# Sigmoid attention in rounds of two pairs of heads: rest keys of both pairs on four 64x64 tiles, queries and keys split from SBUF

## The chip, the core and the metric

One NeuronCore of a Trainium2 chip runs the kernel. The engines named below are TensorE (PE; PEld are its weight loads), VectorE (DVE), ScalarE (ACT), GpSimd (POOL) and SyncE (SP, which issues most DMAs). The metric is the device time of one execution, in microseconds; the kernel before takes 999.67 us (median of three, 999.48 to 1000.31).

## What is computed

Attention with a sigmoid in place of the softmax, over 4 batches of 12 heads with 448 tokens of 64 features, and then two dense layers, each with an inner width of 2048:

```python
scores = scale * np.matmul(q, k.transpose(0, 1, 3, 2)) - np.log(S)
attn = 1.0 / (1.0 + np.exp(-scores))
x = np.matmul(attn, v)              # (4, 12, 448, 64) -> (1792, 768)
h = x @ w_in;  x = np.where(h > 0, h, np.exp(np.minimum(h, 0)) - 1) @ w_out
h = x @ w_in2; x = (h - np.tanh(h)) @ w_out2
```

q, k and v are float32, the weights float64.

## The kernel before

Attention goes by pairs of heads (`pairs`, 24 of them, six per batch). The 448 keys of a head are 3 x 128 keys and a rest of 64 (`RS`). For pair n the kernel does this:

- **Loads.** `ld_qk` brings queries and keys into `raw_qk` (SP's queue); GpSimd puts the two heads side by side into `ql` and `kl` (`side_by_side`, L230), which waits for the transposes of pair n - 2. `ld_kr` and `ld_vr` bring the rest keys and rest values of four pairs at once (`NR`), two DMAs each; `krest` holds head 0 and head 1 in a block diagonal with zeros in the other corners. `ld_v` brings the values of two pairs (`NL`).
- **Transposes** (`transpose`, L299, TensorE): four for the keys (the fourth is the rest), four for the queries, into PSUM.
- **Split.** Each operand becomes two float32r numbers, a head and a rest: `head` (keys on ScalarE, L305; queries on VectorE, L307) copies from PSUM into `es[n % 2]`, and `rest` (VectorE, L312) subtracts the head from the PSUM tile. `es` has two copies, one per parity of the pair.
- **Scores** (`scores`, L334): for each block u of 128 keys three matmuls (head x rest, head x head, rest x head) per head, the two heads on the two 64-row halves of the array. Block u = 3 is the 64 rest keys of both heads on all 128 rows, three matmuls into the bank `psq`. The three score buffers `pss` have two banks each.
- **Sigmoid** (`sig`, L348, ScalarE) on 2 x 448 columns, and on 448 for the rest keys.
- **Values** (`pv`, L359): float32, head 0 into PSUM partitions 0 to 63 and head 1 into 64 to 127 (two column tiles of 128x64); a float32 matmul appears as two instructions in the trace. For u = 3 the rows of `vrest` that belong to the other head are zero.
- **Result** (`xdone`, L371, VectorE) from `psv` into the R tiles, the input of the first dense layer.

TensorE's order in steady state is scores of pair n, transposes of pair n + 2, values of pair n; its tiling goes from 64x128 to 128x128 to 128x64 in each pair.

`Sched` makes the order: every operation has a queue, a cost, what it waits for, and a rank, which in attention is a due time from `PHASES` (nanoseconds from the start of a pair, `CYCLE` apart). Attention is planned first, alone. The dense layers' operations are then put between on all engines, but an operation on ScalarE or VectorE that would delay a planned one of attention by more than `GIVE` is put off. During attention this other work is the narrowing of the float64 weights (`narrow_to`, L534 on ScalarE, L537 and L541 on VectorE), the sums and stores of the first layer's output weights (`p_sum`, L594; `p_store`, L599), whose due times are two `CYCLE`s apart, and, as results come in, the operands of the first products (`x_sum`, L695; `x_head`, L705; `x_rest`, L711; `w_head` and `w_rest`, L668 and L671). The first products (`m_p`, L739) follow the last `pv` on TensorE in a fixed order (`sequence`), 128 rows by 128 columns.

## Time and profile before

| | |
|---|---|
| median of three runs | 999.67 us |
| span of the profiled execution | 997.6 us |
| TensorE busy | 985.6 us (99%) |
| VectorE busy | 763.5 us (77%) |
| ScalarE busy | 601.3 us (60%) |
| GpSimd busy | 105.1 us (11%) |
| TensorE's granted clock | 90% of full speed or more in each of the page's 40 slices |

The profiled execution has its span only, first instruction to last; its time outside the span isn't listed. Busy time is the time in which an engine had at least one instruction running. Records of one engine may overlap: an instruction's recorded time reaches into the next one's start. The weights, the queries, keys and values stream in during the first 125 us, in which the DMA engines are busy nearly throughout.

### The profile page before, as it was taken

How to read it: one execution, taken by the hardware profiler on the slowest of the kernel's cores; microseconds unless marked ns; L12 is line 12 of the kernel's file. 1: busy time of each engine (PE TensorE's matmuls, PEld its weight loads, DVE VectorE, ACT ScalarE, POOL GpSimd, SP SyncE). 2: the span in 40 equal slices, each digit the busy share in tenths (PEclk: the TensorE clock that was granted, in tenths of full speed). 3: DMA queues.
4: the chain of work that ended last, by engine and by line, in shares of the span. 5: the costliest groups of instructions: out<-in, count | busy, mean ns of one | idle time of the engine just before them, and what ended most of it. 6: DMA issues, size and time to landing. Idle time of an engine off the chain costs nothing.

```text
span 997.6 us, 15554 instructions
## 1 busy us (share of the span) xinstructions
PE 985.6 (99%) x5294; PEld 853.5 (86%) x5294; DVE 763.5 (77%) x1155; ACT 601.3 (60%) x966; POOL 105.1 (11%) x118
## 2 busy tenths in 40 slices
...
GB/s 298 294 353 366 307 140 47 56 200 193 193 192 185 188 253 343 396 358 392 379 261 148 231 75 179 178 182 191 196 189 183 323 323 147 126 172 174 127 144 83
DMA packets 144190, 218.60 MB, mean 219 GB/s; under 512 B 21040, under 2 KB 102512, under 8 KB 143856
## 3 DMA queue, kind: packets, MB, share of 16 engines
...
## 4 chain that ended last, share of the span: by engine, by line
PE 96%; DVE 2%; ACT 1%; DMA 0%; issue 0%; SPq 0%; DVEq 0%
PE psa L739 13%; PE psd L739 11%; PE psx L739 10%; PE pvps L359 8%; PE psu L894 7%; PE psv L894 7%; PE psw L894 7%; PE psa L894 6%; PE psb L894 6%; PE psb L739 5%; PE sps L334 5%; PE psy L894 5%; PE psx L894 3%; PE spq L334 2%; PE sps L299 2%; PE psd L894 1%
## 5 line engine op out<-in xcount | busy, mean ns | idle before, releaser
L348 ACT ACTIVATE an<-sps,bias 128x896 f32<-128x896 f32 x72 | 67.6, 1006 | 36.7 <-PE sps L334 36.5
L866 ACT ACTIVATE XB<-t 128x384 fp32r<-128x384 f32 (+1 forms) x111 | 61.9, 562 | 35.1 <-PE psw L894 8.1
L870 DVE TENSOR_TENSOR XB<-t,XB 128x384 fp32r<-128x384 f32 (+1 forms) x111 | 68.1, 624 | 11.2 <-ACT XB L866 11.1
L654 POOL TENSOR_TENSOR second<-second 128x384 f32<-128x384 f32 x15 | 19.0, 1264 | 539.8 <-DVE second L541 406.7
L359 PE MATMUL pvps<-an,vl 128*64 128x448 f32 x288 | 59.4, 548 | 0.0
L334 PEld LDWEIGHTS sps<-e 64*128 64x128 f32 x432 | 39.8, 190 | 19.8 <-PE pvps L359 11.3
L866 ACT ACTIVATE XB<-spare 128x512 fp32r<-128x512 f32 (+1 forms) x72 | 40.9, 573 | 25.8 <-PE psw L894 10.4
L739 PE MATMUL psa<-XB,W 128*128 128x512 f32 x192 | 54.2, 391 | 0.0
L334 PE MATMUL sps<-e 64*128 64x448 f32 x432 | 52.2, 383 | 0.2 <-DVE e L312 0.2
L870 DVE TENSOR_TENSOR XB<-spare,XB 128x512 fp32r<-128x512 f32 (+1 forms) x72 | 44.0, 621 | 7.9 <-ACT XB L866 7.5
L894 PE MATMUL psu<-XB,XB 128*128 128x384 f32 (+1 forms) x192 | 46.3, 348 | 0.0
L894 PE MATMUL psv<-XB,XB 128*128 128x384 f32 (+1 forms) x192 | 46.2, 348 | 0.0
L894 PE MATMUL psw<-XB,XB 128*128 128x384 f32 (+1 forms) x192 | 46.2, 348 | 0.0
L739 PEld LDWEIGHTS psa<-XB,W 128*128 128x128 f32 x192 | 36.0, 188 | 7.5
L768 ACT ACTIVATE spare<-t 128x512 f32<-128x512 f32 (+1 forms) x33 | 19.0, 579 | 36.9 <-DVE t L756 35.9
L359 PEld LDWEIGHTS pvps<-an,vl 128*64 128x64 f32 x288 | 18.5, 136 | 26.0 <-issue 20.1
L654 POOL TENSOR_TENSOR first<-first,second 128x384 f32<-128x384 f32 x30 | 40.1, 1335 | 1.2
L307 DVE CAST e<-sps 128x448 fp32r<-128x448 f32 x24 | 15.0, 623 | 30.8 <-PE sps L299 23.6
L230 POOL COPY first<-raw_qk 128x384 f32<-128x384 f32 (+1 forms) x44 | 25.0, 573 | 117.4 <-PE sps L299 92.6
L739 PE MATMUL psd<-XB,W 128*128 128x512 f32 x144 | 35.7, 391 | 1.5 <-DVE W L671 1.3
L772 ACT ACTIVATE spare<-spare 128x512 f32<-128x512 f32 (+1 forms) x64 | 36.6, 572 | 0.7
L894 PE MATMUL psa<-XB,XB 128*128 128x384 f32 (+1 forms) x156 | 36.9, 347 | 0.0
...
## 6 DMA issues: line engine op xcount, KB each, us to landing
...
```

The source lines that it names most:

```text
L230: nc.gpsimd.tensor_copy(out=(ql, kl)[w][:, n % NL].rearrange("p c (h d) -> p c h d", h=2), in_=x)
L299: nc.tensor.transpose(ps[:, c * P:(c + 1) * P], x, ident[:P, :P])
L334: nc.tensor.matmul(out=ps[:, j, :S], lhsT=e[lanes, ks, cols], rhs=e[lanes, qs, :S], start=(x == 0), stop=(x == 2),)
L348: nc.scalar.activation(out=a[:, :m], in_=T.pop(("s", n, u))[:, :m, :S], func=ACTF.Sigmoid, bias=bias, scale=scale)
L359: nc.tensor.matmul(out=ps[D * j:D * j + D], lhsT=vl[n // NL % NVL][:, n % NL, 3 * j + u] if u < 3 else vrest[n // NR % 2][:, n % NR, j], r ...
L654: by.tensor_tensor(out=out, in0=x, in1=y, op=op)
L739: nc.tensor.matmul(out=ps, lhsT=w[wz][:, k0:k0 + 128], rhs=xs[xz][:, kk], start=(opens and n == 0), stop=(n == 3 * KH - 1), skip_group_che ...
L768: nc.scalar.activation(out=r, in_=h, func=ACTF.Tanh)
L772: nc.scalar.activation(out=r, in_=r, func=ACTF.Exp, scale=-1.0)
L866: nc.scalar.activation(out=at_place(og_place[i, s, p, j], 0, i)[:, :HW[s]], in_=T["graw", i, s, p, j], func=ACTF.Copy)
L870: nc.vector.tensor_tensor(out=lo, in0=T.pop(("graw", i, s, p, j)), in1=f(hi), op=ALU.subtract)
L894: nc.tensor.matmul(out=T["o2", tag], lhsT=lhsT, rhs=rhs, start=(p in OPENS and j == 0 and x == 0), stop=(j == NG - 1 and x == 2), skip_gro ...
```

## The change

Attention goes in rounds of two pairs (`ROUND`). Within a round TensorE does the scores of the first pair, the transposes of both pairs of the next round, the scores of the second pair, the values of both, the rest values of both (`pv_rest`) and the rest scores of both pairs of the next round (`scores_rest`).

- The rest scores are four plain float32 matmuls of 64x64, one per head, on the four quarters of the array, into one score buffer. They take the place of six float32r matmuls. One sigmoid over 2 x 448 columns takes the place of two over 448. The rest values are four matmuls of 64x64 without the zeros; the results of both pairs stand in one tile of two banks, `T["o", m]`, in which the second pair's heads are crossed: partitions 64 to 127 of a bank hold the other pair's head.
- Because of that crossing the first layer's input weights are loaded with the upper 64 rows of neighbouring blocks exchanged, as three DMAs (`load` for `("wi", 0)`).
- The transposes of a pair go into one tile of two banks (the even pair's with the rest keys of both pairs). One copy brings it as float32 into `plain` in SBUF: on VectorE for the even pair (960 columns), on ScalarE for the odd one (832); for pair 0 both engines share it. From there VectorE makes head (`hi`) and rest (`lo`), each over queries and 3 x 128 keys at once, 832 columns. Even transposes use the result's tile, so they wait for both results of the round before; odd ones use a score buffer.
- The bank `psq` is gone; two of the three score buffers lie in the early pool. `an` has five buffers for three. `ld_kr` and `ld_vr` are four DMAs each, all on SP; the zero fills of `krest` and `vrest` are gone.

The diff, cut to its core (a line of "..." marks what is left out):

```diff
-CYCLE = 6900
+CYCLE = 6000
...
+ROUND = 2 * CYCLE
 PHASES = {
-    ("s", 0): 0, ("s", 1): 620, ("s", 2): 1240, ("s", 3): 1900,
-    ("t", 1): 3100 - 2 * CYCLE, ("t", 0): 3500 - 2 * CYCLE, ("pv", 0): 4000, ("pv", 1): 4900, ("pv", 2): 5800, ("pv", 3): 6500,
-    ("sig", 0): 700, ("sig", 1): 1700, ("sig", 2): 2700, ("sig", 3): 3700,
-    ("head", 1): 4400 - 2 * CYCLE, ("head", 0): 4900 - 2 * CYCLE,
-    ("rest", 1): 5050 - 2 * CYCLE, ("rest", 0): 5700 - 2 * CYCLE, ("xdone",): CYCLE + 500,
-    ("ldk",): 4000 - 5 * CYCLE, ("ldqk",): 1000 - 4 * CYCLE, ("side", 1): 4500 - 3 * CYCLE, ("side", 0): 4600 - 3 * CYCLE, ("ldv",): 3300 - 2 * CYCLE,
+    "s": ((0, 600, 1200), (3900, 4500, 5100)), "sig": ((1100, 2100, 3100), (5100, 6100, 7100)),
+    "pv": ((5900, 6650, 7400), (8150, 8900, 9650)), "pvr": 10500, "xdone": (11400, 12000),
+    "sr": -700, "sigr": 50,
+    "t": (2000 - ROUND, 2900 - ROUND), "plain": (2950 - ROUND, 4100 - ROUND), "hi": (4100 - ROUND, 5800 - ROUND), "lo": (4700 - ROUND, 6400 - ROUND),
+    "side": (4500 - 2 * ROUND, 6000 - 2 * ROUND), "ldqk": (7000 - 3 * ROUND, 8500 - 3 * ROUND),
+    "ldk": 5000 - 3 * ROUND, "ldv": 1500 - ROUND,
 }
...
+SHIFTS = {(0, "ldv"): -12000, (0, "sr"): 2550, (0, "sigr"): 2600, (0, "ldvr"): -11000}
...
-    NAN, NAF, NVL, NL, NR = 3, 1, 2, 2, 4
+    NAN, NVL, NL, NR = 5, 2, 2, 4
...
+            plain = [ld_p.tile([128, w], F32, name=f"plain{i}") for i, w in enumerate((DD + EW, EW))]
+            es = [e0.rearrange("p a t -> p (a t)"), ld_p.tile([128, 2 * EW], F32R, name="e1")]
...
+            def rests(w, g):
+                return heads[w][2 * NR * g:2 * NR * (g + 1), KW:S]
 
             def ld_kr(g):
-                for j in range(2):
-                    nc.sync.dma_start(out=krest[g % 2][RS * j:RS * j + RS, :, D * j:D * j + D], in_=rest_of(0, g, j))
+                for y in range(NR):
+                    i, x = divmod(y, 2)
+                    nc.sync.dma_start(
+                        out=krest[g % 2][RS * x:RS * x + RS, i].rearrange("p (h d) -> p h d", h=2),
+                        in_=rests(0, g)[2 * y:2 * y + 2].rearrange("h p d -> p h d"),
+                    )
 
             def ld_vr(g):
-                for j in range(2):
-                    (nc.sync if g else nc.scalar).dma_start(out=vrest[g % 2][RS * j:RS * j + RS, :, j], in_=rest_of(1, g, j))
+                for z in range(2):
+                    for x in range(2):
+                        nc.sync.dma_start(
+                            out=vrest[g % 2][RS * z:RS * z + RS].rearrange("p (i x) d -> x p i d", x=2)[x],
+                            in_=rests(1, g).rearrange("(i x h) p d -> x h p i d", x=2, h=2)[x, z ^ x],
+                        )
...
+            def transpose(n):
+                ps = t_flat(n)
+                for c in range(3):
+                    nc.tensor.transpose(ps[:, DD + c * 128:DD + (c + 1) * 128], kl[:, n % NL, c], ident)
+                if n % 2 == 0:
+                    nc.tensor.transpose(ps[:, :DD], krest[n // NR % 2][:, n // 2 % 2], ident)
                 for c in range(R):
-                    x = krest[n // NR % 2][:, n % NR] if w and c == 3 else t[:, n % NL, c]
-                    nc.tensor.transpose(ps[:, c * P:(c + 1) * P], x, ident[:P, :P])
-
-            def head(n, w):
-                W, slot = ((S, 1), (512, 2))[w]
-                to, x = es[n % 2][:, slot, :W], T["t", n, w][:, :W]
-                if w:
-                    nc.scalar.activation(out=to, in_=x, func=ACTF.Copy)
+                    nc.tensor.transpose(ps[:, DD + KW + c * SP:DD + KW + (c + 1) * SP], ql[:, n % NL, c], ident[:SP, :SP])
+
+            def parts_of(n):
+                lo, hi = DD * (n % 2), DD + EW
+                return [("ACT", lo, DD + KW), ("DVE", DD + KW, hi)] if n == 0 else [(("DVE", "ACT")[n % 2], lo, hi)]
+
+            def to_plain(n, x):
+                by, lo, hi = parts_of(n)[x]
+                at = DD * (n % 2)
+                out, in_ = plain[n % 2][:, lo - at:hi - at], t_flat(n)[:, lo:hi]
+                if by == "ACT":
+                    nc.scalar.activation(out=out, in_=in_, func=ACTF.Copy)
                 else:
-                    nc.vector.tensor_copy(out=to, in_=x)
-
-            def rest(n, w):
-                W, slot, to = ((S, 1, 0), (512, 2, 3))[w]
+                    nc.vector.tensor_copy(out=out, in_=in_)
+
+            def kq(n):
+                return plain[n % 2][:, DD * (1 - n % 2):][:, :EW]
+
+            def hi(n):
+                nc.vector.tensor_copy(out=es[n % 2][:, :EW], in_=kq(n))
+
+            def lo(n):
                 e = es[n % 2]
-                nc.vector.tensor_tensor(
-                    out=e[:, to, :W], in0=T.pop(("t", n, w))[:, :W], in1=f(e[:, slot, :W]), op=ALU.subtract
-                )
+                nc.vector.tensor_tensor(out=e[:, EW:2 * EW], in0=kq(n), in1=f(e[:, :EW]), op=ALU.subtract)
...
+            def scores_rest(m):
+
+                ps = buffer("sr", m)
+                for x in range(2):
+                    for j in range(2):
+                        lanes, c = slice(64 * j, 64 * j + 64), 64 * (j ^ x)
+                        nc.tensor.matmul(
+                            out=ps[c:c + 64, j, :S], lhsT=plain[0][lanes, RS * x:RS * x + RS], rhs=kq(x)[lanes, KW:], start=True, stop=True,
+                        )
+
...
             def pv(n, u):
-                if u == 0:
-                    T["o", n] = psv.tile([128, 512], F32, tag="o", name="pvps")[:, :S]
-                ps = T["o", n]
-
+                m, x = divmod(n, 2)
+                if (x, u) == (0, 0):
+                    T["o", m] = pso.tile([128, 2, BK], F32, tag="o", name="pvps")
                 a = T.pop(("a", n, u))
                 for j in range(2):
                     nc.tensor.matmul(
-                        out=ps[D * j:D * j + D], lhsT=vl[n // NL % NVL][:, n % NL, 3 * j + u] if u < 3 else vrest[n // NR % 2][:, n % NR, j],
-                        rhs=a[:, j if u < 3 else 0], start=(u == 0), stop=(u == 3),
+                        out=T["o", m][D * j:D * j + D, j ^ x, :S], lhsT=vl[m % NVL][:, x, 3 * j + u], rhs=a[:, j], start=(u == 0), stop=False,
                     )
...
+            def pv_rest(m):
+                a = T.pop(("a", m))
+                for x in range(2):
+                    n = 2 * m + x
+                    for j in range(2):
+                        lanes = slice(64 * (j ^ x), 64 * (j ^ x) + 64)
+                        nc.tensor.matmul(
+                            out=T["o", m][D * j:D * j + D, j ^ x, :S], lhsT=vrest[n // NR % 2][lanes, n % NR], rhs=a[lanes, j], start=False, stop=True,
+                        )
...
-                        op("side", n, (w,), "POOL", 1400, side_by_side, [("ldqk", n, w), ("t", n - NL, w)])
-                    op("t", n, (w,), "PE", (420, 440)[w], transpose, loaded("qk"[w], n) + before_s(n - 2, 3))
-                    op("head", n, (w,), ("DVE", "ACT")[w], (620, 600)[w], head, [("t", n, w)] + used)
-                    op("rest", n, (w,), "DVE", (620, 690)[w], rest, [("head", n, w)])
-                for u in range(4):
-                    m2 = width(u) == 2
-                    op("s", n, (u,), "PE", 660, scores, [("rest", n, 0), ("rest", n, 1)] + (before_s(n, u) if u < 3 else [("sig", n - 1, 3)]))
-                    was = ("pv", *divmod(3 * n + u - NAN, 3)) if m2 else ("pv", n - NAF, u)
-                    op("sig", n, (u,), "ACT", 1010 if m2 else 640, sig, [("s", n, u), was])
-                for u in range(4):
-                    op("pv", n, (u,), "PE", 820, pv, [("sig", n, u)] + (loaded("v", n) + [("xdone", n - 1)] if u == 0 else []))
-                before = [("narrow", 3, 2), ("keep", 2, ("wi", 0, 2)), ("keep", 3, ("wi", 0, 3))] if n == 2 * NP else []
-                op("xdone", n, (), "DVE", 680 if pairs[n][0] == 2 else 630, xdone, [("pv", n, 3)] + before)
+                        sch.op(("side", n, w), "POOL", 800, lambda n=n, w=w: side_by_side(n, w), [("ldqk", n, w), ("t", n - NL)], when("side", n) - w)
+                outs_free = [("xdone", n - 4), ("xdone", n - 3)]
+                op(("t", n), "PE", (1000, 850)[x], transpose, loaded("qk", n) + (free_of(("t", n)) if x else outs_free))
+                for y, (by, c0, c1) in enumerate(parts_of(n)):
+                    op(("plain", n, y), by, int(1.06 * (c1 - c0)) + 120 if by == "DVE" else int(0.87 * (c1 - c0)) + 190, to_plain, [("t", n), ("sr", m - 1), ("lo", n - 2)])
+                op(("hi", n), "DVE", 600, hi, copied(n) + [("s", n - 2, u) for u in range(3)])
+                op(("lo", n), "DVE", 1020, lo, [("hi", n)])
+                for u in range(3):
+                    op(("s", n, u), "PE", (800, 750)[x] if u == 0 else 600, scores, [("lo", n)] + free_of(("s", n, u)))
+                    op(("sig", n, u), "ACT", 1010, sig, [("s", n, u), ("pv", *divmod(3 * n + u - NAN, 3))])
+                    opens = copied(2 * m + 2) if (x, u) == (0, 0) and 2 * m + 2 < NPR else []
+                    op(("pv", n, u), "PE", 900 if (x, u) == (0, 0) else 740, pv, [("sig", n, u)] + loaded("v", n) + opens)
+                if x:
+                    op(("sr", m), "PE", 760, scores_rest, copied(n - 1) + copied(n) + free_of(("sr", m)))
+                    op(("sigr", m), "ACT", 1010, sig_rest, [("sr", m), ("pvr", m - 1)])
+                    op(("pvr", m), "PE", 850, pv_rest, [("sigr", m), ("ldvr", n // NR)] + [("pv", n - y, 2) for y in range(2)])
+                    before = [("narrow", 3, 2), ("keep", 2, ("wi", 0, 2)), ("keep", 3, ("wi", 0, 3))]
+                    for y in (n - 1, n):
+                        op(("xdone", y), "DVE", 680 if pairs[y][0] == 2 else 630, xdone, [("pvr", m)] + (before if y == 2 * NP else []))
...
+                    nc.sync.dma_start(out=to[:64], in_=rows.rearrange("(k z p) f -> z p k f", z=2, p=64)[0])
+                    for x in range(2):
+                        nc.sync.dma_start(
+                            out=to[64:].rearrange("p (m x) f -> x p m f", x=2)[x],
+                            in_=rows.rearrange("(m x z p) f -> x z p m f", x=2, z=2, p=64)[1 - x, 1],
+                        )
...
-            sch.chain([("pv", last, 3)] + sequence)
+            sch.chain([("pvr", NPR // 2 - 1)] + sequence)
```

## Rows read from the trace of the kernel before

**Rows 1.** the page: busy time by engine; the chain that ended last

```profile
PE 985.6 (99%) x5294; PEld 853.5 (86%) x5294; DVE 763.5 (77%) x1155; ACT 601.3 (60%) x966; POOL 105.1 (11%) x118
...
PE 96%; DVE 2%; ACT 1%; DMA 0%; issue 0%; SPq 0%; DVEq 0%
```

**Rows 2.** windows: length, busy us (instructions) per engine, clock, DMA share, GB/s

```profile
9.00:26.20 17.20, 16.13 (x93) 9.55 (x92) 7.26 (x13) 9.50 (x12) 4.48 (x8) 1.00 1.03 350
26.20:162.40 136.20, 136.20 (x902) 81.27 (x900) 112.06 (x194) 106.27 (x143) 20.50 (x36) 1.00 0.80 269
162.40:174.50 12.10, 12.10 (x76) 6.30 (x74) 8.38 (x15) 10.30 (x16) 0.00 (x0) 1.00 0.11 34
174.50:200.70 26.20, 24.72 (x119) 21.16 (x118) 25.25 (x41) 18.77 (x36) 5.05 (x4) 1.00 0.16 61
200.70:997.00 796.30, 789.62 (x4084) 729.35 (x4083) 609.65 (x891) 454.39 (x759) 71.95 (x56) 1.00 0.63 216
```

**Rows 3.** timeline of TensorE, one pair: start, us, engine, line, out<-in, count

```profile
80.73 2.09 PE L334 MATMUL sps<-e 64*128 64x448 f32 x18
82.75 0.88 PE L334 MATMUL spq<-e 128*128 128x448 f32 x3
83.46 0.49 PE L299 MATMUL sps<-ident,first 128*128 128x128 f32 x3
...
83.90 0.55 PE L299 MATMUL sps<-ident,first 112*128 112x112 f32 x4
84.38 2.48 PE L359 MATMUL pvps<-an,vl 128*64 128x448 f32 x12
86.68 0.92 PE L359 MATMUL pvps<-a,vrest 128*64 128x448 f32 x4
87.53 0.47 PE L334 MATMUL sps<-e 64*128 64x448 f32 x2
```

**Rows 4.** the same in narrower windows: TensorE, and its weight loads

```profile
81.64 1.17 PE L334 MATMUL sps<-e 64*128 64x448 f32 x10
...
84.81 0.14 PEld L359 LDWEIGHTS pvps<-an,vl 128*64 128x64 f32 x2 [0.23 <-ACT an L348]
85.18 0.14 PEld L359 LDWEIGHTS pvps<-an,vl 128*64 128x64 f32 x2 [0.23 <-issue]
```

**Rows 5.** timeline of VectorE in the same stretch

```profile
87.65 0.62 DVE L371 COPY R0b<-pvps 128x448 f32<-128x448 f32 x1 [0.53 <-PE pvps L359]
88.19 0.95 DVE L541 SCALAR_TENSOR_TENSOR XB<-XB 128x768 int32<-128x768 int32 x1
89.06 0.69 DVE L711 TENSOR_TENSOR XA<-R0a,XA 128x512 fp32r<-128x512 f32 x1
89.66 1.02 DVE L594 TENSOR_TENSOR XB<-XB 128x384 f32<-128x384 f32 x2
91.31 0.62 DVE L307 CAST e<-sps 128x448 fp32r<-128x448 f32 x1 [0.63 <-PE sps L299]
91.85 0.55 DVE L594 TENSOR_TENSOR XB<-XB 128x384 f32<-128x384 f32 x1
92.60 1.22 DVE L312 TENSOR_TENSOR e<-sps,e 128x512 fp32r<-128x512 f32 x2 [0.20 <-ACT e L305]
```

**Rows 6.** VectorE's shift by lines; the timeline where GpSimd and VectorE meet

```profile
L537 DVE TENSOR_SCALAR XB<-XB 128x768 int32<-128x768 int32 x16 | 8.4, 550 | 0.0
...
112.22 0.62 POOL L230 COPY first<-raw_qk 112x512 f32<-112x512 f32 x1 [0.37 <-DMA raw_qk<-in_q_dram]
112.29 1.08 DVE L711 TENSOR_TENSOR XA<-R0b,XA 128x512 fp32r<-128x512 f32 x1
```

**Rows 7.** timeline: SP at the start; VectorE ahead of the end

```profile
7.85 1.29 SPq L237 DMA_DIRECT2D krest<-in_k_dram  x2
...
170.90 0.55 DVE L711 TENSOR_TENSOR R0b<-R1a,R0b 128x384 fp32r<-128x384 f32 x1
...
173.26 0.56 DVE L711 TENSOR_TENSOR R0b<-R1a,R0b 128x384 fp32r<-128x384 f32 x1 [0.62 <-ACT R0b L705]
```

170 lines of the change are left out of this document (84 added, 86 removed).

## The prediction

> **What bounds the kernel now.** I read the page first: TensorE is busy 985.6 us of a span of 997.6, and the chain that ended last is 96% TensorE with 2% VectorE [rows 1]. So a change pays only where it shortens TensorE's own list, and only for as long as nothing else ends later. Next the windows, cut where the stages begin [rows 2]. Attention in steady state is the window from 26.2 to 162.4: twenty pairs in 136.2 us, TensorE never idle, so 6.81 us a pair and 13.62 for two. VectorE is busy 112.06 there, 82%. The reader should then look at the two windows behind. In the last two pairs VectorE has air (8.38 of 12.10). In the 26.2 us after attention's end, where the operands of the first products are still being split, it is busy 25.25, or 96%, while TensorE idles 1.48. There VectorE is already the bound, and whatever it has not finished when attention ends is added to the time one for one. Behind 200.7 TensorE is at 99% and VectorE at 77%: a microsecond won ahead of that point stays won.
>
> The timeline of one pair shows what TensorE spends [rows 3]: scores 80.73 to 82.75 (2.02), rest scores to 83.46 (0.71), transposes to 84.38 (0.92), values to 86.68 (2.30), rest values to 87.53 (0.85), 6.80 in all. Narrower views give the pace inside [rows 4]. Two 64-row score matmuls go side by side: ten take 1.11 us including the change at their end, eighteen 2.02, so a slot of two is 0.20 and about 0.1 is lost at each end. The float32 matmuls with values are two instructions each, and a slot of two column tiles is 0.375 (weight loads at 84.81 and 85.18): eight slots are 3.00 of 3.15, the change costs 0.15. Transposes are 0.11 (128 columns) and 0.095 (112), with 0.10 at the change. A change of tiling thus costs 0.15 to 0.20, and two pairs have six.
>
> **TensorE, part by part, for a round of two pairs.** Scores: the same 18 slots, 18 x 0.2025 = 3.65. Transposes: 15 for 16, seven at 0.11 and eight at 0.095, 1.53. Values: 12 slots x 0.375 = 4.50. Rest values: four matmuls 64x64, eight instructions; if four tiles run at once, two slots, 0.75 where two pairs now spend 1.50. Rest scores: four plain float32 matmuls, 0.75 by the same slot where two pairs now spend 1.42. Changes: into scores 0.20, to transposes 0.20, back 0.20, to values 0.15, to the 64x64 tiles 0.15, none between rest values and the next rest scores: 0.90. Sum 12.08 against 13.62, **1.54 less a round**; a little under half of it is rest values, a little under half rest scores, the remainder changes and the lost transpose.
>
> Ten such rounds give 15.4. The last round has no transposes: 3.65 + 4.50 + 0.75 and three changes of 0.5 together are 9.4; three score buffers now serve seven uses in a row there, so I put 0.6 on it for sigmoids that come late, 10.0 against 12.10 [rows 2]: 2.1. At the start SP issues four DMAs for the rest keys where two took 1.29 us [rows 7], and four for the rest values that ScalarE's queue carried; the loads of pairs 2 and 3 queue behind these, some 3.9 us later (six issues of 0.65), and GpSimd and the second transposes wait for them. Against it stands one shorter round. I take zero, with 2 us either way. TensorE's list is shorter by **17.5 us** at attention's end.
>
> **VectorE, which must keep up.** Its records overlap by 0.08, so I take start to start [rows 5]: 448 columns 0.54 (87.65 to 88.19 and 91.31 to 91.85), 384 columns 0.47, 512 0.60, 768 0.87: 1.04 ns a column on 0.07. Now a pair costs 0.54 (queries' head) + 1.14 (two rests) + 0.54 (copy of the result) = 2.22, a round 4.44. After: one copy of 960 columns out of PSUM 1.07; two heads of 832; two rests of 832 at 0.94; two result copies at 0.54. The head reads and writes SBUF, which no float32 row here does in this form. The nearest is the 768-column shift, one SBUF source, 0.55 [rows 6] where two sources take 0.95 [rows 5]: two elements a cycle. So 0.50, or 0.94 if it goes at one. I take 0.50. Sum 5.03 (5.91 at the other end).
>
> All other VectorE work in the steady window is 11.21 - 4.44 = 6.77 a round. It forms and stores weights and does not shrink. So VectorE needs 11.80 of 12.08, 98%, where it now has 82%. The highest share that a long window shows is the 96% [rows 2]; at that, 11.60 is to be had and 0.20 is missing.
>
> GpSimd's copies come on top. Now they start when the transposes end, while VectorE reads PSUM. One case shows what happens otherwise [rows 6]: a VectorE operation with both sources in SBUF starts 0.07 after a GpSimd copy and takes 1.08 for 0.69. In the new order the first pair's two copies lie beside the copy out of PSUM, the second pair's (0.51 + 0.62 = 1.13) beside heads and rests, which now read SBUF only. Between 0 and 1.13 a round; I take 0.6, since the copy may also be the one that waits. Missing per round: 0.8, ten rounds 8. The last round needs 8.38 - 1.68 - 1.88 = 4.82 (no head and rests, and the four 384-column operations of pair 22 between 170.90 and 173.26 [rows 7] fall behind its end); at 96% of 10.0 that leaves 4.8 to catch up. Backlog 3.2. And the result of pair 22, now copied one pair before attention ends, comes with the last: 0.54 + 4 x 0.47 = 2.4 more in the stage where VectorE is the bound. Given back: **5.6 us**.
>
> The Trainium skill, SBUF — State Buffer, section "SBUF: two separate sides", speaks against this part of the change: VectorE with two SBUF inputs, or in a two-port mode, and GpSimd share a port pair under an exclusive lock, and the one that comes second waits for the whole instruction. The stretched row agrees; by the rule taken strictly the upper end of 1.13 would hold, and the time would be near 993.
>
> ScalarE gets seven full sigmoids for six and two halves, and one copy of 832 columns for two of 512: fewer columns and fewer instructions, and it is busy 78% [rows 2]; no cost. A score buffer's next use waits for its sigmoid, which by the due times in the diff ends some 0.2 us ahead; the even transposes wait for both result copies of the round before, some 1.4 us ahead. Those two are the covers that could fail inside a round. The first layer's weight loads become three DMAs for one, and the rest loads four for two; bytes are the same, and they are issued a round or more ahead, so zero, 2 us if that cover is gone.
>
> **The sum.** Profiled span 997.6; the median of the timed runs is 999.67, 2.1 above it, which I take to be outside the span and unchanged. 999.67 - 17.5 + 5.6 = 987.8, **988 us**.
>
> **The rivals.** *Cover holds*: VectorE packs above 96% and GpSimd is the one that waits; only the moved result is given back or less, with the start gaining up to 2: 980 to 985. For it: the 18% that VectorE idles now is not all lost to waiting. Against it: 98% leaves no room.
>
> *Only two tiles at once*: the 64x64 matmuls run in pairs, so rest scores and rest values cost 1.50 each. A round is 13.58, eleven rounds give back 16.5, and VectorE at 87% keeps up: about 1000, no change. For it: the trace shows two column tiles in step and two row tiles in step, never four. Against it: both kinds of split run fully beside each other.
>
> The Trainium skill, TensorE: Matmul & The Clock Gate, "Part 3: Packing small matmuls — row/col tiling", has matmuls start and end in strict program order, by which the two passes of one tile could hold back the next tile; the same part reports four and more tiles at once. The column pairs in the trace start within one slot, which agrees with the second.
>
> *VectorE sets the round*, the slower side: heads run at one element a cycle and the lock costs its full 1.13. Then a round needs 11.80 + 0.88 + 1.13 = 13.81 of VectorE, 14.39 at 96%; the other work is paced by rounds and shares the in-order queue, so copies and rests for the next round come late and TensorE waits each round. 0.77 a round over ten, less 2.1, plus 2.4: about 1008. It decides from a need of 13.1 a round (0.96 x 13.62). For it: nothing here shows the head's rate. Against it: the shift's 0.55.
>
> **Chances.** Forecast (985 to 993) 0.46; cover holds (980 to 985) 0.21; two tiles at once 0.18; VectorE sets the round 0.15. A measurement of this kernel can tell 0.2%, 2 us. Faster: 0.45 + 0.21 + 0.04 + 0.02 = 0.72. Within: 0.01 + 0.10 + 0.02 = 0.13. Slower: 0.04 + 0.11 = 0.15. Range 980 to 1001: it takes in the first three and leaves out most of the last.
>
> **What would show it.** TensorE: 12.1 us from one round's first scores to the next, eight rest instructions within 0.85 us; at 13.6 the tiles don't run at once. Heads: 0.58 as recorded, or 0.98. VectorE: 95% or more in attention and its operand work running on after the end, with TensorE idle some 6 us more there; if TensorE idles no more than now, the cover held. If TensorE waits inside rounds for copies out of PSUM or result copies, the last rival is on. The forecast is wrong as a whole if the stages behind 200.7 change length.

## The result, and the profile after the change

The changed kernel takes 1008.77 us (median of 4 runs, 1006.06 to 1009.88) where the kernel before took 999.63: a ratio of 1.0087, 95% interval 1.0072 to 1.0102. It is slower by 0.9%; 988 was predicted. The profiled execution took 1009.88, its span is 1008.2.

The page: busy time by engine, and the chain that ended last (it answers [rows 1]).

```profile
PE 977.1 (97%) x5306; PEld 844.7 (84%) x5306; DVE 780.1 (77%) x1143; ACT 597.4 (59%) x943; POOL 112.1 (11%) x110
...
PE 90%; DMA 4%; DVE 2%; ACT 1%; issue 1%; SPq 0%; ACTq 0%; DVEq 0%
```

TensorE is busy 8.5 us less and the span is 10.6 longer. DMA, 0% of the chain before, now holds 4% of it. The windows say where (length; busy us and count for TensorE, its weight loads, VectorE, ScalarE, GpSimd; TensorE's granted clock; DMA share; GB/s). They answer [rows 2]:

```profile
25.33:61.53 36.20, 36.20 (x278) 20.55 (x274) 31.35 (x42) 28.05 (x31) 9.38 (x13) 1.00 0.93 301
61.53:72.31 10.78, 6.89 (x41) 5.55 (x39) 5.99 (x10) 5.19 (x6) 1.99 (x4) 0.68 0.86 250
105.33:116.68 11.35, 6.62 (x39) 5.28 (x37) 5.87 (x12) 6.84 (x9) 0.71 (x2) 0.70 1.04 374
...
171.23:209.70 38.47, 27.26 (x122) 23.06 (x119) 36.71 (x64) 25.07 (x48) 5.30 (x4) 0.91 0.14 52
209.70:1004.00 794.30, 791.17 (x4084) 730.43 (x4083) 610.25 (x891) 453.94 (x758) 71.90 (x56) 1.00 0.64 216
```

From 25.33 to 61.53 three rounds run in 36.20 us without a gap: 12.07 each. Then there are two holes, in both of which TensorE works for 6.6 to 6.9 of about 11 us at a mean clock of 0.7. Attention ends at 171.3, before at 174.6: 3.3 us gained, where 17.5 were predicted. The next step of the first layer begins at 209.70 instead of 200.7, so the stretch behind the end has grown from 26.2 to 38.5 us, VectorE's work in it from 25.3 to 36.7. All that follows is 4084 instructions in both.

**The round is as computed.** TensorE's timeline (start, us, line, out<-in, count), beside [rows 3]:

```profile
23.66 0.98 PE L397 MATMUL pvps<-ar,vrest 64*64 64x448 f32 x8
24.47 0.54 PE L369 MATMUL sps<-plain 64*64 64x448 f32 x2
24.48 0.54 PE L369 MATMUL sps<-plain,plain 64*64 64x448 f32 x2
24.84 0.54 PE L369 MATMUL sps<-plain 64*64 64x448 f32 x2
24.86 0.54 PE L369 MATMUL sps<-plain,plain 64*64 64x448 f32 x2
```

The four tiles start together, at 24.47 and again at 24.84. From the rest values to the rest scores and on to the next scores (25.33) eight instructions take 0.81 and 0.86 us.

**The holes come from weights.** ScalarE's waits from 20 to 130 us (who <- whom: us in total, times, longest), and SP's issues before the first hole:

```profile
ACT XB L598 <- DMA XA<-in_moe_w_out_dram: 6.7, 2, 4.7
ACT R1b L598 <- DMA R1a<-in_moe_w_in_dram: 6.4, 1, 6.4
...
ACT R1b L598 <- DMA kept_wi<-R1b: 2.2, 1, 2.2
```

```profile
52.27 1.97 SPq L663 DMA_DIRECT2D p_forms<-XB  x1
54.35 3.92 SPq L242 DMA_DIRECT2D vrest<-in_v_dram  x4
58.38 0.59 SPq L580 DMA_DIRECT2D R1a<-in_moe_w_in_dram  x1
59.70 1.76 SPq L582 DMA_DIRECT2D R1a<-in_moe_w_in_dram  x2
61.51 2.56 SPq L234 DMA_DIRECT2D krest<-in_k_dram  x4
```

Four loads of rest values take SP 3.92 us; behind them stand the three pieces of a first weight, the last of them issued by 61.46. ScalarE reached the narrowing of that weight at 58.6 and waits 6.4 us, until 65.06, with the sigmoids of the next round behind it in its queue. Before the change the same view has one line, a wait for TensorE, and none for a weight:

```profile
ACT an L348 <- PE sps L334: 27.4, 17, 4.8
```

On TensorE the first hole of the changed kernel looks like this:

```profile
61.53 1.49 PE L358 MATMUL sps<-e 64*128 64x448 f32 x12
66.90 1.49 PE L358 MATMUL sps<-e 64*128 64x448 f32 x6 [3.89 <-ACT ar L375]
68.32 0.90 PE L312 MATMUL sps<-ident,first 128*128 128x128 f32 x3
```

A gap of 3.89 us for a sigmoid, and behind it three transposes in 0.90 us that take 0.49 to 0.55 elsewhere: the granted clock is at 0.5 (the 1.2 GHz level) for 6.8 us. The second hole has a gap of 4.73, for a load of the output weights (XA). In sum attention idles 9.7 us in gaps of over 0.1 us, against 1.1 before; the rest of the lost 14 us goes with the clock.

Behind the end TensorE waits 11.2 us, 1.5 before. The two longest of its waits there:

```profile
PE psd L803 <- ACT R1b L815: 7.2, 1, 7.2
PE psd L803 <- ACT R0a L732: 1.8, 1, 1.8
```

The ScalarE copy that releases the first had itself waited 2.1 us for VectorE's last subtraction of the second token block's operands (R1a, L775).

### The profile page after: what moved, and what is told of

Its sections match the earlier page's. It is cut to its first block, busy times and chain, and to the rows that moved or that the text cites. A ratio compares the mean times of both kernels' runs of the same rounds, so it can differ in the third digit from the quotient of the medians.

```text
span 1008.2 us, 15604 instructions
## 1 busy us (share of the span) xinstructions
PE 977.1 (97%) x5306; PEld 844.7 (84%) x5306; DVE 780.1 (77%) x1143; ACT 597.4 (59%) x943; POOL 112.1 (11%) x110
## 4 chain that ended last, share of the span: by engine, by line
PE 90%; DMA 4%; DVE 2%; ACT 1%; issue 1%; SPq 0%; ACTq 0%; DVEq 0%
PE psa L803 13%; PE psd L803 12%; PE psx L803 10%; PE psu L958 7%; PE psv L958 7%; PE psw L958 7%; PE psa L958 6%; PE psb L958 6%; PE psb L803 5%; PE psy L958 5%; PE sps L358 4%; PE pvps L387 4%; PE psx L958 3%; PE psd L958 1%; DMA XB<-in_moe_w_out_dram 1%; DMA vl<-in_v_dram 1%
## 5 line engine op out<-in xcount | busy, mean ns | idle before, releaser
L930 ACT ACTIVATE XB<-t 128x384 fp32r<-128x384 f32 (+1 forms) x111 | 62.0, 562 | 37.5 <-PE psw L958 9.9
L934 DVE TENSOR_TENSOR XB<-t,XB 128x384 fp32r<-128x384 f32 (+1 forms) x111 | 68.3, 626 | 11.4 <-ACT XB L930 11.1
L379 ACT ACTIVATE an<-sps,bias 128x896 f32<-128x896 f32 x72 | 68.6, 1008 | 3.7 <-PE pvps L387 2.0
L358 PE MATMUL sps<-e 64*128 64x448 f32 x432 | 55.1, 395 | 9.7 <-ACT ar L375 9.3
L930 ACT ACTIVATE XB<-spare 128x512 fp32r<-128x512 f32 (+1 forms) x72 | 41.1, 573 | 27.0 <-PE psw L958 11.2
L387 PE MATMUL pvps<-an,vl 128*64 128x448 f32 x288 | 56.8, 543 | 0.0
L226 POOL COPY first<-raw_qk 128x384 f32<-128x384 f32 (+1 forms) x44 | 34.2, 798 | 109.1 <-DMA raw_qk<-in_k_dram 79.5
L832 ACT ACTIVATE spare<-t 128x512 f32<-128x512 f32 (+1 forms) x33 | 19.0, 579 | 36.9 <-DVE t L820 35.9
L958 PE MATMUL psb<-XB,XB 128*128 128x384 f32 (+1 forms) x156 | 36.8, 347 | 0.0
```

Source lines behind the costliest of these rows:

```text
L226: nc.gpsimd.tensor_copy(out=(ql, kl)[w][:, n % NL].rearrange("p c (h d) -> p c h d", h=2), in_=x)
L358: nc.tensor.matmul(out=ps[:, j, :S], lhsT=e[lanes, EW * kz + u * 128:EW * kz + (u + 1) * 128], rhs=e[lanes, EW * qz + KW:EW * qz + EW], st ...
L379: nc.scalar.activation(out=a, in_=T.pop(("s", n, u))[:, :, :S], func=ACTF.Sigmoid, bias=bias, scale=scale)
L387: nc.tensor.matmul(out=T["o", m][D * j:D * j + D, j ^ x, :S], lhsT=vl[m % NVL][:, x, 3 * j + u], rhs=a[:, j], start=(u == 0), stop=False,)
L832: nc.scalar.activation(out=r, in_=h, func=ACTF.Tanh)
L930: nc.scalar.activation(out=at_place(og_place[i, s, p, j], 0, i)[:, :HW[s]], in_=T["graw", i, s, p, j], func=ACTF.Copy)
```

## The experiments

"End" is the end of attention's last product, "idle" the sum of TensorE's gaps of over 0.1 us that begin between 9 us and there, "stretch" the time from the end to the next step, with VectorE's busy time in it. All are of the profiled execution. Times are medians; ratios are to the kernel before on the same chip. Kernels with late weights spread by up to 8 us from run to run (e5: 998.6 to 1006.5), so end, idle and stretch, which come from one execution, stand for that execution: in e5 and e6 it is the fastest one.

| run | end | idle | stretch (VectorE) | us | ratio |
|---|---|---|---|---|---|
| before | 174.6 | 1.1 | 26.1 (25.2) | 999.6 | |
| after | 171.3 | 9.7 | 38.4 (36.7) | 1008.8 | 1.0087 |
| e1 pace | 172.7 | 11.9 | 38.7 (35.8) | 1008.2 | 1.0087 |
| e2 latencies | 165.9 | 8.8 | 39.7 (36.2) | 1003.6 | 1.0044 |
| e3 issues as before | 155.9 | 0.6 | 39.1 (35.4) | 993.2 | 0.9941 |
| e6 rest loads only | 155.7 | 2.1 | 38.2 (36.7) | 996.9 | 0.9968 |
| e5 merged q, k loads | 162.3 | 2.9 | 37.5 (36.9) | 1002.1 | 1.0031 |
| e12 before, more issues | 184.8 | 7.6 | 26.1 (25.3) | 1009.1 | 1.0086 |
| e4 no GpSimd copies | 172.2 | 10.4 | 38.4 (36.7) | 1008.0 | 1.0092 |
| e7 sums on GpSimd | 172.1 | 10.0 | 38.8 (37.5) | 1008.1 | 1.0083 |
| e8 e5 + both blocks' sums | 170.8 | 10.1 | 38.3 (36.7) | 1009.0 | 1.0097 |
| e11 gap filled | 172.3 | 11.4 | 37.9 (35.7) | 1008.0 | 1.0083 |
| e9 rest loads by GpSimd | 164.3 | 6.2 | 38.6 (37.4) | 1004.1 | 1.0044 |
| e10 e9 + 12 copies moved | 167.1 | 7.7 | 34.6 (33.4) | 1001.4 | 1.0025 |
| e13 + weights by GpSimd | 163.6 | 3.8 | 38.7 (35.6) | 1003.3 | 1.0048 |
| e14 e13 + 12 copies | 170.1 | 4.9 | 35.0 (33.4) | 1002.1 | 1.0023 |
| e15 e13 + 4 copies | 168.4 | 5.4 | 33.8 (32.7) | 998.8 | 0.9994 |
| e16 combined | 169.3 | 8.4 | 34.5 (33.4) | 999.5 | 1.0006 |
| e17 e16, longer plan | 161.8 | 4.3 | 35.7 (34.1) | 997.3 | 0.9982 |
| e18 e17, one load longer | 170.8 | 9.7 | 35.8 (34.1) | 1003.5 | 1.0034 |

### Why the weights are late: pace, order or issues

**e1.** The weights' due times at the old pace.

```diff
-fixed[k] = (2 * k[1] + 2) * CYCLE
+fixed[k] = (2 * k[1] + 2) * 6900      # and the first weights' likewise
```

> The changed kernel, with the due times of the weight work (loads, narrowing, sums, stores) spread over rounds of 6900 ns a pair again, as before the change; attention itself keeps 6000. The changed kernel asks for the same bytes 13% sooner, and the DMA engines are full until 117 us. Theory 'pace' (the transfers are late because their demand was pulled forward): ScalarE's waits for weights (6.4, 4.7, 2.2 and 2.0 us there) shrink below 1 us each, TensorE's idle time before the end of attention falls from 9.4 us to under 3, no half-clock stretch is left in it, attention ends at 157 to 162 us instead of 171.2, and the time falls to 993 to 1003. Theory 'issues' (SP issues more DMAs, one behind the other): one or more waits of over 2 us remain, attention still ends at 166 or later, time 1003 to 1010. Theory 'VectorE backlog' (whatever attention gains is given back behind it): attention ends sooner, but the step behind it still begins at 205 or later, time 1004 to 1010.

1008.2 us, all gaps still there (4.7, 2.6, 4.3 us), as 'issues' had it: the pace isn't the cause.

**e2.** Only the latencies that the order is planned by.

```diff
-p_load ... 11000      +p_load ... 17000
-load (place 4) 8500   +load (place 4) 14000
```

> The changed kernel, with only the latencies that the order of the work is planned by made longer: 17 us instead of 11 for the second weights' loads and 14 instead of 8.5 for the first weights'. The loads are issued at about the same times, but ScalarE's narrowing stands further back in its queue. Theory 'order' (the narrowing stands ahead of sigmoids although its load is late, 5 to 7 us by the trace): TensorE's idle time inside attention falls from 9.4 us to under 3 and attention ends at 157 to 162 us; time 993 to 1004, by as much as VectorE gives back. Theory 'pace' (the engines of the DMA are short by a sum of bytes that no order mends): the waits come back later in the stretch until 117 us, attention ends at 166 or later, 1003 to 1010.

1003.6. The early gap is gone, but one of 7.2 us came at 99, and attention ends at 165.9: the signs of 'order' didn't come. Room in the order helps, it doesn't remove the lateness.

**e3.** As many issues as before.

```diff
-for y in range(NR): ... rests(0, g)[2 * y:2 * y + 2]       # 4 loads
+for x in range(2): ... rests(0, g)[NR * x:NR * x + NR]      # 2; values likewise
-to[:64] and two parts of to[64:]                             # 3 loads
+to                                                           # 1
```

> The changed kernel with as many DMA issues as before the change: each rest load of four pairs is two DMAs instead of four (of the wrong heads, so which rest keys and values meet is left out), each first weight load is one instead of three (the exchange of its rows is left out). Bytes are the same. 24 + 24 + 12 issues become 12 + 12 + 4. Theory 'issues': SP is free some 20 us sooner in sum before 160 us, the loads are issued on time, ScalarE's waits fall below 1 us each, attention ends at 157 to 162, time 993 to 1003. Theory 'pace': SP is freer, but the transfers still land late: at least one wait of over 2 us, attention ends at 165 or later, time 1003 to 1010.

993.2 us, ratio 0.9941 (0.9926 to 0.9956): 15.6 us off the changed kernel's median, 14.6 by the ratios, with the same bytes. The kernel brings the wrong rests together, so only its time counts. Its windows up to the end, and behind it:

```profile
9.00:155.90 146.90, 146.11 (x1078) 81.89 (x1078) 127.92 (x186) 115.87 (x135) 30.56 (x44) 1.00 0.88 292
155.90:195.04 39.14, 29.22 (x118) 24.58 (x118) 35.40 (x64) 24.99 (x48) 4.69 (x4) 0.83 0.15 55
```

TensorE is busy for 146.1 of 146.9 us. Cutting the loads up, more issues for the same bytes, is the cause of the holes; the stretch behind the end is untouched.

**e6.** Of those the rest loads alone (the weights keep three pieces).

> The changed kernel with the rest loads alone as two DMAs for four pairs instead of four (of the wrong heads, so which rest keys and values meet is left out); the first weight loads keep three issues each with their rows exchanged. 24 issues fewer. Theory 'issues': nearly all of the gain of the run that had both (993.2): 992 to 998, attention ends at 156 to 161. Rival (the three-piece weight load, whose second and third piece stood 1.3 and 2.5 us behind the first, is what ScalarE waits for): the wait of 6.4 us for the first weights stays, 4 us or more of idle time inside attention, time 998 to 1006.

996.9 (0.9968, 0.9954 to 0.9983): the rest loads carry most of it, about 12 us, the weights' pieces some 3 to 4.

**e5.** Other issues taken away: queries, and keys, of both pairs of a round in one load.

```diff
-nc.sync.dma_start(out=(qraw, kraw)[w][:, n % NL], in_=x)          # 4 a round
+nc.sync.dma_start(out=(qraw, kraw)[w].rearrange("p i h x -> p (i h) x"), in_=x)   # 2
```

> The changed kernel with the queries and keys of both pairs of a round loaded by one DMA each: two issues a round instead of four, 20 fewer in all, the same bytes; rest loads and first weight loads keep their many issues, and what is computed is the same. Theory 'issues' (SP's queue of issues, each 0.5 to 2 us, delays what stands behind it): it doesn't matter which issues go; TensorE's idle time inside attention falls from 9.7 to under 3 us, attention ends at 156 to 161, time 992 to 999. Rival (the rest loads or the three-piece weight loads themselves are the slow transfers): idle inside attention stays above 6 us, attention ends at 166 or later, time 1002 to 1010.

1002.1 (1.0031): 6.7 us gained by issues that have nothing to do with weights or rests, less than expected. One wait of 4.4 us for a first weight is left. Its pieces were issued at 24.70 to 28.53, ahead of four rest loads that took SP 6.6 us, and landed at 37.4.

**e12.** The kernel before, with its loads cut up as the change does it.

```diff
-rest_of(0, g, j)                    # 2 loads for four pairs, values likewise
+rest_of(0, g, j)[:, c]              # 4, c = two pairs
+to[:64], to[64:, :3], to[64:, 3:]   # a first weight in three loads
```

> The kernel before the change with the loads cut up as the change cuts them: rest loads of four pairs as four DMAs instead of two, first weight loads as three instead of one; same bytes, same result, nothing else. Theory 'issues alone': ScalarE starts to wait for weights, TensorE's idle time in attention grows from 1.1 to 4 us or more, time 1003 to 1010. Theory 'issues and pace' (only the faster rounds leave SP no room): with 13% more time a round SP's extra 20 to 25 us fit; idle in attention under 2.5 us, time 998 to 1002.

1009.1 us, 1.0086 (1.0069 to 1.0104). The cut-up loads alone, without the faster rounds, cost the old kernel as much as the whole change did. Its windows and its waits of ScalarE:

```profile
9.00:184.80 175.80, 168.22 (x1070) 98.56 (x1069) 128.92 (x221) 125.71 (x170) 26.61 (x44) 0.98 0.78 248
184.80:210.94 26.14, 24.65 (x119) 21.08 (x118) 25.27 (x41) 18.69 (x36) 5.06 (x4) 1.00 0.16 60
```

```profile
ACT R1b L544 <- DMA R1a<-in_moe_w_in_dram: 6.6, 1, 6.6
```

Attention ends 10.2 us later; the stretch behind it keeps its 26.1.

**What an issue costs.** SP's issues up to 160 us took 77.2 us before the change, 101.3 after, 97.6 in e12, 84.6 in e3 and e6. Besides, SP waits ahead of an issue for earlier transfers of its own that have nothing to do with that load:

```profile
SPq L259 <- DMA XB<-in_moe_w_out_dram: 3.3, 3, 1.8
...
SPq L222 <- DMA XA<-in_moe_w_out_dram: 2.3, 2, 1.6
```

Here loads of values and queries wait for weights. In the trace SP's transfers count up eight semaphores by turns, and each issue waits first for the one that it is to use, which the transfer eight issues earlier raises: up to 160 us of the changed kernel no issue finds more than eight of SP's transfers under way. Cut into smaller pieces, eight are fewer bytes. These waits were 14.2 us (20 of them) from 9 to 150 us before, 30.4 (43) after and 30.3 (36) in e12; from 9 to 120 us the DMA engines moved 340 GB/s before, 298 after, 339 in e3. But e6 has 28.5 us of such waits and runs almost without a hole, so no sum foretells a stall.

Whether a late load was issued late or took long is in the traces. From issue to landing, the load of the same first weight in the changed kernel (issued from 58.4), in e12 (from 45.0) and, in one piece, before (from 42.4):

```profile
DMA to landing us min/median/max: 4.1/4.5/5.1
DMA to landing us min/median/max: 11.1/12.1/14.1
DMA to landing us min/median/max: 8.7/8.7/8.7
```

In the changed kernel the pieces were quick and had been issued too late; the load of the second hole took 6.8 us, such loads 7.0 to 10.6 before. In e12 they went out 3.7 to 8.4 us ahead of the narrowing and took long, as in e5 (11.1 to 11.4 us). So late weights come both ways: by what stands ahead of an issue, and by slow transfers. What makes these slow, the eight under way or the DMA engines, wasn't told apart.

### VectorE, GpSimd and the stretch behind the end

**e4.** GpSimd's copies cut to a corner.

```diff
-nc.gpsimd.tensor_copy(out=to, in_=x)
+nc.gpsimd.tensor_copy(out=to[:, :1, :, :8], in_=x[:, :1, :, :8])
```

> The changed kernel with GpSimd's copies that lay queries and keys side by side cut to 8 of 64 columns of one block (the rest of the copying is left out). Where GpSimd copied, VectorE's copies into head halves took 832 ns instead of 595, its subtractions 1322 instead of 1024. Theory 'lock' (that contention makes the backlog of VectorE and, through late stores in SP's queue, the late loads too): VectorE's work until the step behind attention falls by 5 to 9 us, TensorE's idle time behind attention falls from 10 us by at least half, time 995 to 1003. Theory 'pace': VectorE gains the same 5 to 9 us, but ScalarE's waits for weights stay over 4 us and attention ends at 168 or later; time 1001 to 1008.

VectorE's work from 9 us to the end falls by 10.0 us (131.9 to 121.9), some 0.9 a round, and nothing else changes: 1008.0 us, the stretch 38.4 with 36.7 of VectorE in it. What VectorE does behind the end is fixed by the order, which is written out when the kernel is built; a VectorE that is done sooner has the same 36.7 us left there.

**e7.** The sums of the second token block on GpSimd.

```diff
 def sums_on(i, s, x):
-    return "DVE"
+    return "POOL" if (i, s) == (0, 1) else "DVE"
```

> The changed kernel with the 12 subtractions of 384 columns that form the second token block's sums (some 5.9 us of VectorE behind attention) on GpSimd; nothing else changes, the stalls inside attention stay. Theory 'backlog in the order' (behind the end VectorE has 36.7 us of work that the order puts there, where it had 25.3 in the same stretch before): TensorE's idle time behind the end falls from 11.2 to 4 to 7 us, the stretch from the end to the next step from 38.5 to 31 to 35 us, time 1000 to 1006. Rival (ScalarE, whose copies TensorE waits for by name there, is late for itself): the 7.2 us gap stays, the stretch is 37 or longer, time 1007 to 1011. Rival (lock: GpSimd's subtractions slow VectorE's down beside them by what they relieve): the stretch is 36 to 40, time 1006 to 1012.

38.8 us, 1008.1: both rivals' numbers fit, and the rows decide for the lock. VectorE's subtractions of 384 columns, and GpSimd's beside them:

```profile
192.08 6.51 DVE L775 TENSOR_TENSOR XB<-R1a,XB 128x384 fp32r<-128x384 f32 x5
```

```profile
188.04 3.57 POOL L759 TENSOR_TENSOR R1a<-R1a 128x384 f32<-128x384 f32 x3
191.56 4.05 POOL L759 TENSOR_TENSOR R1b<-R1b,R1a 128x384 f32<-128x384 f32 x3
```

1.30 us each, 0.48 to 0.55 without GpSimd: what GpSimd took over it cost again. The Trainium skill, SBUF — State Buffer, "SBUF: two separate sides", has the port pair locked for a whole instruction when VectorE reads two SBUF inputs while GpSimd reads SBUF; these rows agree.

**e8.** e5 with both blocks' sums on GpSimd.

> The changed kernel with both: one load a round for the queries and one for the keys of two pairs, and the sums of both token blocks of the first layer on GpSimd (24 subtractions off VectorE, some 13 us). If both causes are right, attention ends at 156 to 161, TensorE idles under 8 us behind it, no half-clock stretch inside attention, time 982 to 992, ahead of the kernel before the change. If GpSimd's subtractions, 1.3 to 1.6 us each by the order's own table, are what TensorE then waits for, or slow VectorE down, 992 to 1000. If the queue of issues isn't the cause of the stalls, 1000 or more.

1009.0, where 982 to 992 were hoped for; 1000 or more was to speak against the queue of issues. A first weight is late again (a hole of 3.6 us at 39), and with more on GpSimd the transposes wait 3.5 us for VectorE's result copies, as they never did in the changed kernel. Behind the end nothing is gained, so the run tells little of the issues.

**e11.** The 7.2 us gap filled with 30 discarded products.

```diff
+for _ in range(30):
+    nc.tensor.matmul(out=spare_bank, lhsT=at_place("W1", 0, i)[:, :128], rhs=xo(i, s, "T1", 0)[:, 0], start=True, stop=True)
```

> The changed kernel with 30 discarded products of 384 columns (0.195 us each, 5.9 us) put on TensorE into the gap of 7.2 us behind attention's end; their results go to a bank that nobody reads. Theory 'clock follows the gap': the granted clock stays at its full level in the stretch of 6.8 us that was at half behind that gap, the 18 products after it take 0.17 to 0.2 us apiece instead of up to 0.5, the step behind begins 1.5 to 2.5 us sooner, time 1005 to 1008. Rival (the clock falls there for another reason): the half-clock stretch stays where it was.

TensorE with the gap filled, and then as it was:

```profile
199.46 5.50 PE L802 MATMUL psu<-R0b,W 128*128 128x384 f32 x30 [0.94 <-ACT W L732]
205.75 0.62 PE L807 MATMUL psd<-XB,R0a 128*128 128x384 f32 x2 [0.79 <-ACT R1b L819]
206.21 0.35 PE L807 MATMUL psd<-XB,R0b 128*128 128x384 f32 x1
```

```profile
204.46 1.01 PE L803 MATMUL psd<-XB,R0a 128*128 128x384 f32 x2 [7.21 <-ACT R1b L815]
205.27 0.52 PE L803 MATMUL psd<-XB,R0b 128*128 128x384 f32 x1
```

The clock stays at its full level, and a pair takes 0.62 us for 1.01. Yet the stretch is only 0.5 us shorter, where 1.5 to 2.5 were expected: a wait of 0.86 us for ScalarE opens behind the faster products. The clock follows the gap, as expected; its price there was covered by the same backlog.

### Off SP's queue, and off VectorE

**e9.** Most rest loads issued by GpSimd.

```diff
-nc.sync.dma_start(
+(nc.gpsimd if g > 1 else nc.sync).dma_start(
```

> The changed kernel with the rest loads from the third group of four pairs on (32 issues) issued by GpSimd instead of SP; bytes, pieces and what is computed are the same. Theory 'issues' (what stands behind them in SP's queue is late): ScalarE's waits for weights fall under 2 us in sum, TensorE's idle time in attention from 9.7 to under 3 us, attention ends at 156 to 161; behind it as before, time 992 to 1000. Rival (the many small pieces fill the DMA engines themselves, whoever issues them): idle in attention stays above 6 us, attention ends at 166 or later, 1002 to 1010. Rival (GpSimd, which also copies queries and keys, is late with those): a wait for the transposes' inputs shows up, 998 to 1010.

1004.1, better by 4.7 but short of the forecast; idle stays at 6.2 us, as the first rival had it. One hole is left, of 5.8 us at 39. SP's rows ahead of it:

```profile
29.22 5.63 SPq L242 DMA_DIRECT2D vrest<-in_v_dram  x4
35.14 0.60 SPq L580 DMA_DIRECT2D R1a<-in_moe_w_in_dram  x1
35.78 1.28 SPq L582 DMA_DIRECT2D R1a<-in_moe_w_in_dram  x2
```

That group of rest values had stayed on SP; the first weight behind it takes 4.7 to 6.5 us from issue to landing, and lands 7.3 us after ScalarE asks for it. The Trainium skill, DMA: Bandwidth & Descriptors, "Issuing engines are not separate DMA queues", says that issuing from several engines only saves the sequencer's time, usually small beside the transfer. Here the move, on the path of a late load, is worth 4.7 us; GpSimd's transfers count up semaphores of their own, so SP's eight are relieved as well, and which of the two it was isn't shown.

**e10.** e9 with the odd pairs' result copies on ScalarE.

```diff
+if n % 2 == 1:
+    nc.scalar.activation(out=to, in_=from_, func=ACTF.Copy)
```

> The same with the result copies of the odd pairs on ScalarE too: 12 copies of 0.62 us, 7.4 us, off VectorE inside attention, which the order may fill with operand work that it now puts behind the end. Theory 'backlog in the order': the stretch from attention's end to the next step shortens by 3 to 6 us against the run without it, its idle time from 11 to 5 to 8 us, time 3 to 6 us below that run's. Rival (the stretch's length is set by something else than the amount of VectorE's work, as its 7.2 us gap has come out the same in six kernels): the stretch keeps its 38 us and the time is the same within 1.5 us. Rival (ScalarE, at 78%, is full with them): sigmoids come late, attention ends later by 2 us or more.

```profile
167.10:201.74 34.64, 26.80 (x118) 22.40 (x119) 33.45 (x57) 26.56 (x52) 5.01 (x4) 0.90 0.16 57
```

7.4 us taken off VectorE shorten the stretch by 4.0, as expected. ScalarE waits for VectorE's copy of the even pair before several of its own, and a hole of 6.7 us stays at 63; at 1001.4 the time is 2.7 us below e9's, not 3 to 6.

**e13.** Rest loads and first weights off SP.

```diff
+(nc.gpsimd if g >= 1 else nc.sync)      # values; keys from g >= 2; first weights nc.gpsimd
```

> The changed kernel with the rest loads (from the second group of values, the third of keys on) and the three-piece loads of the first weights issued by GpSimd; bytes, pieces and what is computed are the same. Theory 'SP's queue' (a load is late when it stands behind others there): no stall over 2 us is left, TensorE's idle time in attention under 2 us, attention ends at 155.5 to 158, the stretch behind it 38 us as in all runs of the changed kernel, time 992 to 998. Rival (the pieces, whoever issues them, or GpSimd's own queue, with its copies): a stall of 3 us or more stays, attention ends at 161 or later, time 999 to 1006.

1003.3, with attention's end at 163.6: the rival's numbers. From 11 us on the longest hole is 2.2 us, now from the second weights' loads on SP. But attention gets going 4 us later (first rest values at 27.7, not 23.7), most of which the idle column doesn't hold:

```profile
10.02 0.45 PE L314 MATMUL sps<-ident,krest 128*128 128x128 f32 x1 [3.67 <-DMA krest<-in_k_dram]
```

GpSimd, free from the start, issues the first weight at 1.45, ahead of the first rest keys. SP issues these from 1.66, as in the changed kernel, and they land after 7.1 to 7.6 us instead of 2.3 to 3.9. Late transfers are not only a matter of SP. e14 and e15 have the same late start (a gap of 4.6 and 4.3 us).

**e14, e15.** e13 with 12, or with the last 4, result copies on ScalarE.

> The same, and the result copies of the odd pairs on ScalarE (12 of 0.62 us). Theory 'backlog': the stretch behind attention's end shrinks from 38 to 34 to 35.5 us, as it did where GpSimd had the rest loads alone, and the time is 2 to 4 us below the run without: 988 to 995. Rival (ScalarE's copies wait for VectorE's of the even pair and hold up sigmoids): attention ends 2 us later or more, which takes it back: 992 to 998.

> The same as the first of these, and only the result copies of the last two rounds (4 of 0.62 us, 2.5 us) on ScalarE. Theory 'backlog' (the stretch shrinks by the work that leaves VectorE, one for one): 1.5 to 2.5 us off the stretch, time 990 to 996, between the other two. Rival (it is where the work is taken from that counts: in the last rounds VectorE was busy throughout, before that it had idle time anyway): as much off the stretch as with 12 copies, 3 to 4 us.

1002.1 and 998.8, both above their ranges, with attention's end 6.5 and 4.8 us later than in e13. Four copies out of the last two rounds shorten the stretch by 5.0 us, 12 spread over all by 3.8: as much and more, as e15's rival had it. Its reason doesn't hold. VectorE in the last two rounds, in e13 and in e15:

```profile
140.50:163.60 23.10, 23.05 (x170) 11.79 (x160) 20.13 (x31) 19.10 (x25) 0.00 (x0) 1.00 0.38 129
145.10:168.40 23.30, 23.23 (x172) 11.77 (x160) 21.76 (x35) 18.27 (x23) 0.00 (x0) 1.00 0.37 128
```

It isn't busy throughout, but 87% in e13. Two of the four copies stood in these rounds, two behind the end. In e15 VectorE is without them and yet busy 93%: the order, made anew, put other work there, which then doesn't stand behind the end. In these two executions the next step begins at 202.3 and 202.2, as what the stretch gained the end lost; the gain of 4.6 us is one of the medians.

**e16.** e5, the rest loads by GpSimd, and e15's four copies.

> The changed kernel with three things: the queries, and the keys, of both pairs of a round in one load each; the rest loads (from the second group of values, the third of keys on) issued by GpSimd; the result copies of the last two rounds on ScalarE. What is computed is the same. SP has 20 + 32 issues fewer, the first weights' loads keep three pieces on SP. Theory 'SP's queue': idle in attention under 3 us, attention ends at 156 to 160, the stretch behind it 33.5 to 35 us, time 988 to 995, ahead of the kernel before. Rival (the first weights' three pieces are late by themselves, or the DMA engines are slow with pieces whoever issues them): one stall of 3 us or more stays, attention ends at 161 or later, time 996 to 1002.

999.5. The first weights are late again (10.3 us of waits): the rival.

**e17.** The same, planned for 15 and 10 us of latency.

> The same, with the order planned for longer loads: 15 us instead of 11 for the second weights, 10 instead of 8.5 for the first weights. If the stalls that are left come from narrowing that stands in ScalarE's queue ahead of a load that is a few us late, they go: idle in attention under 1.5 us, attention ends at 156 to 158, time 987 to 993, at or below the first run's. If the loads are only later still by then, no difference within 1.5 us.

997.3 us, ratio 0.9982 (0.9970 to 0.9994): the best with the same result, just ahead of the kernel before, but short of 987 to 993. One hole of 3.6 us at 39 is left.

**e18.** e17 with that one load planned at 14 us.

> The combined version with the second load of the first weights planned at 14 us (9 us for the other three, 15 for the second weights'); what is computed is the same. Its narrowing stands some 9 us later in ScalarE's queue; the load behind it on the same buffer goes out later too. Theory 'order': the stall of 3.6 to 4.9 us at 39 us is gone, idle in attention under 2 us, attention ends at 156 to 160, the stretch behind it 34 to 36 us, time 989 to 995. Rival (the lateness moves on to the next load, which now has 9 us): a stall of 3 us or more at 58 to 64 us, attention ends at 161 or later, time 996 to 1001.

1003.5: the lateness moved on to the next load, a hole of 5.5 us at 69 (ScalarE waits 7.7 us for it), and 4.1 us of gaps for GpSimd's copies came in addition. No order that was tried is free of late weights; what of it is SP, what the DMA engines, stays open.

## Why the prediction was wrong

**The round: right.** 12.07 us against 12.08; eight rest instructions in 0.81 and 0.86 against 0.75; four tiles at once. With the issues taken back (e3) attention ends at 155.9; the prediction had 157.0.

**VectorE's rates: right.** One head clear of GpSimd's copies and one beside them:

```profile
54.15 0.60 DVE L335 CAST e<-plain 128x832 fp32r<-128x832 f32 x1
...
55.40 2.13 POOL L226 COPY first<-raw_qk 128x384 f32<-128x384 f32 x3 [6.04 <-PE sps L358]
...
55.72 0.90 DVE L335 CAST e<-plain 128x832 fp32r<-128x832 f32 x1
```

0.60 clear (0.58 said), copies of 960 columns 1.16 and rests 1.02 as recorded (1.07 and 0.94 were start to start, to which a record adds 0.08).

**The cover costed at nothing: the step that failed.** The prediction set the three pieces for one and four for two at zero, "2 us if that cover is gone", since "bytes are the same, and they are issued a round or more ahead". Bytes were the wrong measure and a round ahead was no cover: the first weight's load was issued at 58.38 to 61.46 us for a narrowing that stood at 58.6. It cost 14.3 us at attention's end (171.3 against 157.0), 9.7 of it idle time, the rest mostly clock, and e12 shows it without any of the change's rounds: 10.2. Of the covers inside a round that the prediction named, the even transposes' held; the sigmoid's, 0.2 us, gave way only where ScalarE stood still for a weight. What failed is a third one, ScalarE's queue, which has weights in it. Of some 22.5 us between the predicted and the profiled span these loads are 14.3, the next term 6.7 and the stages behind it 1.6.

**What VectorE gives back: the direction right, the size half.** 5.6 us were said, 12.3 came (38.4 less 26.1). The work did go behind the end, 11.5 us of it. But the term let VectorE be busy 96% in each of ten rounds and took only what didn't fit. The sign it gave, 95% or more in attention, didn't come: 81% in the changed kernel, 87% in e3. e3 by rounds, the first and the next nine:

```profile
24.35:36.42 12.07, 12.07 (x95) 6.84 (x91) 8.05 (x10) 10.77 (x12) 3.27 (x4) 1.00 1.05 322
36.42:144.92 108.50, 108.50 (x823) 61.70 (x819) 100.87 (x150) 85.91 (x99) 20.81 (x32) 1.00 0.93 316
```

VectorE is busy 67% and 93%. At 96% these ten rounds would have held 6.8 us more, an estimate from these two lines; 6.7 is what the term lacks. The runs show in its place: what is left behind the end is set by the order and not by VectorE's speed (e4: 10.0 us freed, nothing gained), and moving four copies in the order changes it (e15). With the issues mended and this as it is, the time is 993.2; the prediction's 988 lacks the rest here.

**The lock: the size in range, the effect not.** 0.6 a round was taken from 0 to 1.13; e4 shows some 0.9. In the kernel with its holes it moved the time by nothing measurable; without them it wasn't tried.

**The clock had no term.** Stretches of 3.4 to 10.2 us at half clock follow the holes. One of 3.4 us at 625 goes with the 1.6 us by which the stages from the next step on are longer (798.5 us against 796.9; 796.5 in e3): the six profiles with such a stretch at 618 to 627 are the six in which these stages are longest. It stands behind a gap of 1.28 us that the kernel before has too, without the fall, so nothing here ties it to the change.

**The rivals.** "VectorE sets the round" gave 1008, near the time measured, but its mechanism isn't in the trace: no round waits for a copy out of PSUM, and heads run at 0.60. That its number is so near is luck. The slower side came from a mechanism that no rival held.
